# Attention, top-1 routing and a two-layer network in one kernel: where the first slot's row load and the w_in conversions stand

## The chip, the cores and the metric

The kernel runs on one core of one Trainium2 chip. The metric is device time in microseconds (us), the median of three timed runs; smaller is better. Nothing else runs on the chip.

## What is computed

The reference, cut to what matters here (all float32 unless said otherwise):

```python
# attention: 4 batches, 8 heads, 576 positions, head size 64
x = attention(q, k, v)                       # downsampled by 4 + a local band, summed
x = x.transpose(0, 2, 1, 3).reshape(2304, 512)
# one expert of eight for each token
e_idx = argmax(x @ w_gate + modality_bias[modality_id], axis=1)
for e in range(8):
    mask = e_idx == e
    h = np.maximum(x[mask] @ w1[e], 0.0)     # 512 -> 1024
    out[mask] = gate_w[mask, None] * (h @ w2[e])
# a dense network over all tokens; w_in (512 x 2048) and w_out arrive as float64
h = out @ w_in
g = np.maximum(h, 0.0) + alpha * np.minimum(h, 0.0)
return g @ w_out
```

## The kernel before

The program has three stages, one after the other on TensorE (PE).

**Attention and routing.** For each tile of 96 tokens the attention output is formed, the expert is chosen, and the row (512 values and its gate weight) is scattered by an indirect DMA into a table `xs` in device memory, sorted by expert. While this runs, five "early" blocks of 128 rows of the fullest expert are computed as filler (class `Early`: eight times an `ActivateRelu` of a first product, `eh<-ph`, then four copies `eo<-py` on ScalarE (ACT), then a store). At the end `Router.plan` works on one partition of VectorE (DVE): from the row counts it makes a table `r_tab` that says for each slot which expert and which rows it has, and a flag `r_rare` for a division of rows that does not fit the common case. The first slot's few numbers are cast into a small table of their own (`r_tab_109`) near the plan's start.

**Seven slots of 256 rows.** `slot(s)` takes 256 rows of one expert. Rows come by four DMAs (`L<-xs`, after a fill of zeros `xs<-z`), are scaled on GpSimd (POOL, `L<-L`), transposed on DVE (`T<-L`) and split into two fp32r parts: `xh` by a cast on ACT, `xl` by a subtraction on DVE (helper `split`). Weights are split in the same way: `w1h`, `w2h` on ACT, `w1l` on DVE, `w2l` on DVE or POOL. Each slot has 96 matmuls into `h` and 96 into `y`; ACT and DVE make `hh` and `hl` from `h`. A block that runs only if `r_rare` is set (`with tc.If(rare>0): every()`) stands between the stages, and all engines jump over it.

**The dense network**, five blocks of 512 rows (`moe2`), all PE.

w_in is float64. `W2in(i)` makes one of 32 pieces of 128 x 256: a DMA brings the raw words (`wi<-in_moe_w_in`, three buffers), three integer operations on DVE join them to a float32 (`xwi`, two buffers), ACT casts the high part (`wih<-xwi`) and POOL subtracts for the low part (`wil<-xwi,wih`). All 32 must be done before the dense network. `AT0=8` pieces are written in the program before the jump, six more in each of the slots 0 to 3.

Each engine takes its instructions in one order, fixed when the program is built; a scheduler sets it from the data dependencies and from priorities (`tc.high_priority`). DMAs are issued by SyncE (SP) in order too. Memory of a pool that is closed is given to pools opened later, and the first writer there waits for the last user of the old tile.

The functions that the change touches:

Of the kernel before, what the change touches and what calls it, by code (L numbers as in the profile page):

```python
# [8 lines left out]
B,H,S,D=4,8,576,64  # L9
# [6 lines left out]
def attention(ctx, tc, q, k, v, mod, wg, bias, xs, running, ps, eps, zeros, filler):  # L16
# [297 lines left out]
    def gate3(b,t):  # L314

        x,ng,oh=st.pop((b,t))
        p=psum([TT,E],f"rk{b}{t}")
        nc.tensor.matmul(p,lhsT=tri,rhs=oh,start=True,stop=False)
        nc.tensor.matmul(p,lhsT=ones,rhs=running[0],start=False,stop=False)
        nc.tensor.matmul(p,lhsT=ones[0:1],rhs=eoff,start=False,stop=True)  # L320
        old=running[0]
        running[0]=new_running(b*NT+t)
        nc.gpsimd.tensor_tensor(out=running[0],in0=old,in1=oh,op=ALU.add)
# [50 lines left out]
LEAD=1; WLOAD=tuple([0, 0, 1, 2, 2, 3, 3, 4]); EARLY=tuple([3, 6, 10, 14, 16]); AT0=8  # L374
F=1024; F2=2048; SL=256; SE=128; NSP=len(EARLY); NK=N//SL; NSU=-(-(N-SE*NSP)//SL); NSM=N//SL+E-1
ENG=mybir.EngineType

class Router:

    def __init__(self, tc, rp, cp):  # L380
# [18 lines left out]
        self.one=c([TT,1],"r_one",BF16); nc.gpsimd.memset(self.one,1.0)  # L399
        self.A=c([1,E,E],"r_A"); self.X=c([1,7,E],"r_X")  # L400
# [5 lines left out]
    def counts(self, psum, running):  # L406
        p=psum([1,E],"cnt")
        self.nc.tensor.matmul(p,lhsT=self.one,rhs=running[0],start=True,stop=True)
        return p
# [31 lines left out]
    def plan(self, psum, running, cp):  # L441
# [16 lines left out]
        nc.vector.tensor_tensor(out=left[:,0:1],in0=left[:,0:1],in1=dn,op=ALU.subtract)  # L458
# [25 lines left out]
        v=w([1,7,NSM,E],"v")  # L484
        nc.vector.tensor_tensor(out=v,in0=u[:,0:1].to_broadcast([1,7,NSM,E]),in1=X[:,:,None,:].to_broadcast([1,7,NSM,E]),op=ALU.mult)
        y=w([1,7,NSM],"y")
        nc.vector.tensor_reduce(out=y,in_=v,axis=AX.X,op=ALU.add)
# [49 lines left out]
def split(nc, hi, lo, x, lo_engine):  # L537

    nc.scalar.copy(hi,x)  # L539
    lo_engine.tensor_tensor(out=lo,in0=x,in1=hi.bitcast(F32),op=ALU.subtract)  # L540
# [11 lines left out]
class Rows:  # L552
# [26 lines left out]
class Early:  # L579
# [3 lines left out]
    def start(self, k, xr):  # L583
# [15 lines left out]
        for c in range(4):  # L599
            for f in range(8):  # L600
                S.append(lambda f=f,c=c: mm(("y",c),w.r2[:,f,128*c:128*c+128],h[:,f],f==0,f==7))
            S.append(lambda c=c: nc.scalar.copy(o[:,c],get(("y",c))))
# [5 lines left out]
def moe(tc, stack, router, wts, rows, ep, fp, W2in):  # L608
# [5 lines left out]
    xin={}  # L614
# [5 lines left out]
    def prep_x(s, name=""):  # L620
        L=xin[s]; T=rows.turn(wk,L,f"{name}{s}",SL)
        if name:
            hi=fp.tile([128,4,512],F32R,tag="xh",name=f"xh{name}{s}")[:,:,:SL]; lo=fp.tile([128,4,512],F32R,tag="xl",name=f"xl{name}{s}")[:,:,:SL]
        else:
            hi=wk.tile([128,4,SL],F32R,tag="xh",name=f"xh{name}{s}"); lo=wk.tile([128,4,SL],F32R,tag="xl",name=f"xl{name}{s}")
        split(nc,hi,lo,T,nc.vector)
        xin[s]=(hi,lo)
# [8 lines left out]
    W1={}; W2={}  # L636
# [36 lines left out]
    def slot(s):  # L673
        last=s+1==NSU
        if s==0: load_x(1)
# [11 lines left out]
        for f in range(8):  # L687
# [10 lines left out]
            nc.vector.scalar_tensor_tensor(out=hl,in0=h,scalar=0.0,in1=hh.bitcast(F32),op0=ALU.max,op1=ALU.subtract)  # L698
            H.append((hh,hl))
            if 2<=f<7: two(f-2)  # L700
            if f<6: W2in(AT0+6*s+f)
# [94 lines left out]
def body(tc,q,k,v,mod,wg,bias,w1,w2,w_in,w_out,alpha,out):  # L796
    nc=tc.nc
    with ExitStack() as ctx:
# [10 lines left out]
        with ExitStack() as a:  # L809
            cp=a.enter_context(tc.tile_pool(name="plan",bufs=1))  # L810
            router=Router(tc,rp,cp)
            running=[None]
# [16 lines left out]
            tmp=a.enter_context(tc.tile_pool(name="plan_work",bufs=1))  # L829
            with tc.high_priority(500): router.plan(psum,running,tmp)  # L830
# [17 lines left out]
        with ExitStack() as s1:  # L848
            def W2in(i):
                c,p=divmod(i,8); c=3-c; ps=slice(256*p,256*p+256)  # L850
                if c<0: return
                r=wst.tile([128,256,2],I32,tag="raw64",name=f"wi{c}{p}")
                nc.sync.dma_start(r.rearrange("p d w -> p (d w)"),w_in[128*c:128*c+128,ps].bitcast(I32))
                from64(nc,wst,f"wi{c}{p}",wir[:,c,ps],wil[:,c,ps],r,nc.gpsimd)
# [3 lines left out]
            first0()  # L858
            for i in range(AT0): W2in(i)
            with tc.If(rare>0): every()  # L860
# [33 lines left out]
```

## Time and profile before

| | us |
|---|---|
| median of three timed runs | 880.58 (879.72 to 883.82) |
| the profiled execution | 883.92 |
| its span | 882.2 |
| PE busy (92% of the span) | 814.7 |
| DVE busy (60%) | 530.3 |
| ACT busy (41%) | 360.6 |
| POOL busy (30%) | 261.8 |

A busy time is the sum of an engine's instructions over the whole span, across stages with different limits; what an engine waits for must be read from the stretch in question. In the rows further down a number in square brackets is the engine's idle time just ahead of an instruction, with what ended it.

### The profile page before, as it was taken

How to read it: one execution, taken by the hardware profiler on the slowest of the kernel's cores; microseconds unless marked ns; L12 is line 12 of the kernel's file. 1: busy time of each engine (PE TensorE's matmuls, PEld its weight loads, DVE VectorE, ACT ScalarE, POOL GpSimd, SP SyncE). 2: the span in 40 equal slices, each digit the busy share in tenths (PEclk: the TensorE clock that was granted, in tenths of full speed). 3: DMA queues.
4: the chain of work that ended last, by engine and by line, in shares of the span. 5: the costliest groups of instructions: out<-in, count | busy, mean ns of one | idle time of the engine just before them, and what ended most of it. 6: DMA issues, size and time to landing. Idle time of an engine off the chain costs nothing.

```text
span 882.2 us, 16794 instructions
## 1 busy us (share of the span) xinstructions
PE 814.7 (92%) x6175; PEld 698.2 (79%) x6175; DVE 530.3 (60%) x1302; ACT 360.6 (41%) x863; POOL 261.8 (30%) x450
## 2 busy tenths in 40 slices
PE   5787899899995699999999999999999999999997
PEld 3565687678895589889999888888888888888895
DVE  6856756656336799996755998443344333533361
ACT  8688795885322465565652233211121111111120
POOL 9325555365423645543321332100010001000100
PEclk9888789999999699999999999999999999999999
DMA  7635666322235434537401352200020001000000
GB/s 198 164 95 162 182 186 160 98 56 66 66 89 108 110 86 92 150 101 208 112 25 52 113 171 73 93 4 0 1 81 10 0 1 55 13 0 1 37 13 25
DMA packets 96611, 71.77 MB, mean 81 GB/s; under 512 B 40456, under 2 KB 83976, under 8 KB 96520
## 3 DMA queue, kind: packets, MB, share of 16 engines
q1 hardware_dynamic: 93544, 61.02, 25.8%
q0 software_dynamic: 2976, 9.59, 3.2%
q8 instruction: 51, 0.84, 0.4%
q14 instruction: 40, 0.33, 0.1%
HBM read 76.43 MB, written 18.90 MB: 108 GB/s over the span
## 4 chain that ended last, share of the span: by engine, by line
PE 57%; DVE 3%; DMA 2%; issue 2%; SPq 0%; POOL 0%; POOLq 0%; ACT 0%; DVEq 0%; ACTq 0%
PE oh L770 23%; PE oy L761 22%; PE h L695 7%; PE y L714 5%; DVE w2l L540 1%; DMA L<-xs 1%; DMA wi<-in_moe_w_in 1%; DVE w1l L540 1%; DVE xwi L548 1%; DVE hl L698 0%; DMA ytok<-L 0%; DMA oT<-ysT 0%; DMA out<-o,ti 0%; DVE xwi L549 0%; DVE oxl L540 0%
## 5 line engine op out<-in xcount | busy, mean ns | idle before, releaser
L539 ACT CAST gh<-m 128x512 fp32r<-128x512 f32 (+1 forms) x80 | 44.5, 556 | 241.6 <-DVE m L773 241.6
L770 PE MATMUL oh<-oxh,wil 128*128 128x512 f32 (+1 forms) x320 | 118.9, 372 | 0.0
L770 PE MATMUL oh<-oxh,wih 128*128 128x512 f32 (+1 forms) x320 | 118.9, 371 | 0.0
L770 PE MATMUL oh<-oxl,wih 128*128 128x512 f32 (+1 forms) x320 | 118.6, 371 | 0.0
L772 DVE TENSOR_SCALAR m<-oh,al 128x512 f32<-128x512 f32 (+1 forms) x80 | 55.5, 694 | 92.2 <-PE oh L770 92.2
L787 POOL DMA_INDIRECT out<-o,ti x18 | 17.6, 976 | 308.9 <-ACT o L786 271.3
L761 PE MATMUL oy<-woh,gh 128*128 128x512 f32 x272 | 107.1, 394 | 0.0
L761 PE MATMUL oy<-wol,gh 128*128 128x512 f32 x272 | 106.7, 392 | 0.0
L761 PE MATMUL oy<-woh,gl 128*128 128x512 f32 x272 | 106.4, 393 | 0.0
L695 PE MATMUL h<-xh,w1h 128*128 128x256 f32 x224 | 66.4, 297 | 15.2 <-DVE hl L698 7.9
L540 DVE TENSOR_TENSOR gl<-m,gh 128x512 fp32r<-128x512 f32 (+1 forms) x80 | 48.9, 612 | 40.1 <-ACT gh L539 40.0
L770 PEld LDWEIGHTS oh<-oxh,wil 128*128 128x128 f32 x320 | 60.2, 188 | 11.8
L770 PEld LDWEIGHTS oh<-oxh,wih 128*128 128x128 f32 x320 | 60.1, 188 | 11.5
L770 PEld LDWEIGHTS oh<-oxl,wih 128*128 128x128 f32 x320 | 60.1, 188 | 11.3
L695 PE MATMUL h<-xl,w1h 128*128 128x256 f32 x224 | 65.4, 292 | 0.0
L695 PE MATMUL h<-xh,w1l 128*128 128x256 f32 x224 | 65.1, 291 | 0.0
L714 PE MATMUL y<-hh,w2h 128*128 128x256 f32 x224 | 61.8, 285 | 0.7 <-ACT hh L697 0.7
L761 PEld LDWEIGHTS oy<-woh,gl 128*128 128x128 f32 x272 | 51.1, 188 | 12.0
L714 PE MATMUL y<-hl,w2h 128*128 128x256 f32 x224 | 59.6, 285 | 0.9 <-DVE hl L698 0.9
L714 PE MATMUL y<-hh,w2l 128*128 128x256 f32 x224 | 60.2, 285 | 0.0
L761 PEld LDWEIGHTS oy<-wol,gh 128*128 128x128 f32 x272 | 51.0, 188 | 11.4
L761 PEld LDWEIGHTS oy<-woh,gh 128*128 128x128 f32 x272 | 51.1, 188 | 11.0
(303 smaller groups left out, 1874.1 us busy)
## 6 DMA issues: line engine op xcount, KB each, us to landing
wraw<-in_moe_w SPq DMA_DIRECT2D x56, 512.0 KB
wi<-in_moe_w_in SPq DMA_DIRECT2D x32, 256.0 KB
wo<-in_moe_w_out SPq DMA_DIRECT2D x32, 256.0 KB
vw<-in_v SPq DMA_DIRECT2D x88, 64.0 KB
xs<-z SPq DMA_DIRECT2D x8, 528.0 KB
ldq<-in_q SPq DMA_DIRECT2D x16, 256.0 KB
ldk<-in_k SPq DMA_DIRECT2D x16, 256.0 KB
ldv<-in_v SPq DMA_DIRECT2D x8, 512.0 KB
```

Of the source, the lines that this page charges most:

```text
L539: nc.scalar.copy(hi,x)
L540: lo_engine.tensor_tensor(out=lo,in0=x,in1=hi.bitcast(F32),op=ALU.subtract)
L548: nc.vector.scalar_tensor_tensor(out=xi,in0=lw,scalar=29,in1=xi,op0=ALU.logical_shift_right,op1=ALU.bitwise_or)
L695: nc.tensor.matmul(h,lhsT=a[:,c],rhs=b[:,c],start=n==0,stop=n==11); n+=1
L714: nc.tensor.matmul(y,lhsT=a[:,f],rhs=b,start=n==0,stop=n==23); n+=1
L761: nc.tensor.matmul(y[t],lhsT=a[:,ts],rhs=b[:,f],start=f==0 and k==0,stop=f==15 and k==2)
L770: nc.tensor.matmul(h[:,:n],lhsT=a[:,c,fs],rhs=b[:,c,:n],start=k==0,stop=k==11); k+=1
L772: nc.vector.tensor_scalar(out=m[:,:n],in0=h[:,:n],scalar1=0.0,scalar2=al[:,f:f+1],op0=ALU.min,op1=ALU.mult)
L787: nc.gpsimd.indirect_dma_start(out=out[:],out_offset=bass.IndirectOffsetOnAxis(ap=ti[:,t:t+1],axis=0),in_=o[:],in_offset=None,bounds_check ...
```

## The change

Six edits. The plan's work tiles come out of the pool `plan` and no longer out of a pool opened for them (`plan_work`), and the table `v` of the plan is made in two parts. The load and preparation of the first slot's rows are traced at high priority. `AT0` goes from 8 to 4, so that slot 4 has the last four pieces of w_in. The pieces ahead of the jump are tied (`issue_after`) behind the first slot's load (on SP) and behind its `xl` (on DVE); those inside a slot are tied behind the `hl` of their step and behind the load of slot 1's rows. A raw piece of w_in is now loaded two pieces ahead of its conversion. Each engine gets one prefetch hint for the jump, placed behind an instruction of its own.

```diff
-LEAD=1; WLOAD=tuple([0, 0, 1, 2, 2, 3, 3, 4]); EARLY=tuple([3, 6, 10, 14, 16]); AT0=8
+LEAD=1; WLOAD=tuple([0, 0, 1, 2, 2, 3, 3, 4]); EARLY=tuple([3, 6, 10, 14, 16]); AT0=4
...
-        v=w([1,7,NSM,E],"v")
-        nc.vector.tensor_tensor(out=v,in0=u[:,0:1].to_broadcast([1,7,NSM,E]),in1=X[:,:,None,:].to_broadcast([1,7,NSM,E]),op=ALU.mult)
+        v=w([1,4,NSM,E],"v")
         y=w([1,7,NSM],"y")
-        nc.vector.tensor_reduce(out=y,in_=v,axis=AX.X,op=ALU.add)
+        for a,z in ((0,4),(4,7)):
+            nc.vector.tensor_tensor(out=v[:,:z-a],in0=u[:,0:1].to_broadcast([1,z-a,NSM,E]),in1=X[:,a:z,None,:].to_broadcast([1,z-a,NSM,E]),op=ALU.mult)
+            nc.vector.tensor_reduce(out=y[:,a:z],in_=v[:,:z-a],axis=AX.X,op=ALU.add)
...
     def first():
-        with tc.high_priority(0): load_x(0); L=xin[0]; prep_x(0)
+        with tc.high_priority(450): load_x(0); L=xin[0]; prep_x(0)
+        loaded=rows.loaded
         rows.tokens(L,router.reg(2,0,[ENG.SP],N),SL)
+        return loaded,turned[0]
...
-        if s==0: load_x(1)
+        if s==0: load_x(1); after[0]=rows.loaded
...
-            if f<6: W2in(AT0+6*s+f)
+            if f<6:
+                with tc.issue_after(d.ins), tc.issue_after(after[0].ins): W2in(AT0+6*s+f)
...
-            tmp=a.enter_context(tc.tile_pool(name="plan_work",bufs=1))
-            with tc.high_priority(500): router.plan(psum,running,tmp)
+            with tc.high_priority(500): router.plan(psum,running,cp)
+        early.go(len(early.steps)-10)
+        mark=early.mark
         early.finish()
...
+            def W2in_load(i):
+                c,p=divmod(i,8); c=3-c
+                if c<0: return
+                r=staged["in",i]=wst.tile([128,256,2],I32,tag="raw64",name=f"wi{c}{p}")
+                return nc.sync.dma_start(r.rearrange("p d w -> p (d w)"),w_in[128*c:128*c+128,256*p:256*p+256].bitcast(I32))
             def W2in(i):
+                W2in_load(i+2)
                 c,p=divmod(i,8); c=3-c; ps=slice(256*p,256*p+256)
-                if c<0: return
-                r=wst.tile([128,256,2],I32,tag="raw64",name=f"wi{c}{p}")
-                nc.sync.dma_start(r.rearrange("p d w -> p (d w)"),w_in[128*c:128*c+128,ps].bitcast(I32))
-                from64(nc,wst,f"wi{c}{p}",wir[:,c,ps],wil[:,c,ps],r,nc.gpsimd)
+                if c>=0: from64(nc,wst,f"wi{c}{p}",wir[:,c,ps],wil[:,c,ps],staged.pop(("in",i)),nc.gpsimd)
+            W2in_load(0); router.marks[ENG.SP]=W2in_load(1)
+            router.marks[ENG.Activation]=mark; router.marks[ENG.Pool]=running[1]
...
-            first0()
-            for i in range(AT0): W2in(i)
-            with tc.If(rare>0): every()
+            a=first0()
+
+            for e,i in router.marks.items():
+                with tc.issue_after(i.ins): tc.mark_branch_hint_location("rare",engines=(e,))
+            with tc.issue_after(a[0].ins), tc.issue_after(a[1].ins):
+                for i in range(AT0): W2in(i)
+            with tc.If(rare>0,label="rare"): every()
```

The order in which the built program issues its instructions changes at three places. First SP, from the raw loads of w_in behind the last tile's work to the load of the first slot's rows. Before:

```order
L853 DMA wi_4462<-in_moe_w_in 128x512
L853 DMA wi_4470<-in_moe_w_in 128x512
L853 DMA wi_4478<-in_moe_w_in 128x512
L512 TENSOR_LOAD r_tab_109 x2
L559 ISA
L559 DMA xs<-z 1024x1x132
L853 DMA wi_4486<-in_moe_w_in 128x512
L853 DMA wi_4494<-in_moe_w_in 128x512
L577 DMA ysT<-eo_3428 128x4x128
L512 TENSOR_LOAD r_tab_109
L564 ISA
L564 DMA L_4446<-xs 32x8x132
```

Of the change:

```order
L861 DMA wi_4412<-in_moe_w_in 128x512
L861 DMA wi_4414<-in_moe_w_in 128x512
L907 BRANCH_PREFETCH_HINT
L514 TENSOR_LOAD r_tab_109 x2
L561 ISA
L561 DMA xs<-z 1024x1x132
L514 TENSOR_LOAD r_tab_109
L566 ISA
L566 DMA L_4448<-xs 32x8x132
```

The two raw loads and the store that stood between the fill of zeros and the rows now come behind the rows.

Second ACT, the last instructions ahead of the jump: activations and copies of the last early block (`eh`, `eo`), the cast of the first slot's rows (`xh`) and casts of w_in (`wih`). Before:

```order
L598 ACTIVATE eh_3763<-ph_3924 128x128
L539 CAST wih<-xwi_4496 128x256
L602 COPY eo_3764<-py_4005 128x128
L539 CAST xh_4454<-T_4452 128x1024
L539 CAST wih<-xwi_4504 128x256
L602 COPY eo_3764<-py_4037 128x128
L539 CAST wih<-xwi_4512 128x256
L602 COPY eo_3764<-py_4047 128x128
L539 CAST wih<-xwi_4520 128x256
L602 COPY eo_3764<-py_4128 128x128
L539 CAST wih<-xwi_10130 128x256
L539 CAST wih<-xwi_10160 128x256
```

Of the change:

```order
L601 ACTIVATE eh_3763<-ph_3889 128x128
L541 CAST xh_4456<-T_4454 128x1024
L601 ACTIVATE eh_3763<-ph_3912 128x128
L601 ACTIVATE eh_3763<-ph_3918 128x128
L601 ACTIVATE eh_3763<-ph_3924 128x128
L541 CAST wih<-xwi_4471 128x256
L541 CAST wih<-xwi_4479 128x256
L605 COPY eo_3764<-py_4005 128x128
L605 COPY eo_3764<-py_4037 128x128
L541 CAST wih<-xwi_4487 128x256
L541 CAST wih<-xwi_4495 128x256
L605 COPY eo_3764<-py_4047 128x128
```

Behind these stand the copy `eo_3764<-py_4128`, the hint, the load of the flag and the branch. The cast of the rows has moved from behind the first copy to ahead of the sixth activation, and four casts of w_in stand ahead of the jump where ten stood.

Third DVE, its first instructions behind the jump: the low parts of slot 0's weights (`w1l`, `w2l`), the joining of w_in (`xwi`) and the first `hl`. Before:

```order
L549 SCALAR_TENSOR_TENSOR xwi_10193<-wi_10191,xwi_10193 128x256
L540 TENSOR_TENSOR w1l_0_10100<-wraw,w1h_0_10099 128x512
L547 TENSOR_SCALAR xwi_10228<-wi_10226 128x256
L540 TENSOR_TENSOR w1l_1_10104<-wraw,w1h_1_10103 128x512
L548 SCALAR_TENSOR_TENSOR xwi_10228<-wi_10226,xwi_10228 128x256
L540 TENSOR_TENSOR w1l_2_10108<-wraw,w1h_2_10107 128x512
L549 SCALAR_TENSOR_TENSOR xwi_10228<-wi_10226,xwi_10228 128x256
L540 TENSOR_TENSOR w2l_20_10346<-wraw,w2h_20_10345 128x512
L540 TENSOR_TENSOR w1l_3_10137<-wraw,w1h_3_10136 128x512
L698 SCALAR_TENSOR_TENSOR hl_0_10125<-h_0_10111,hh_0_10124 128x256
```

Of the change:

```order
L542 TENSOR_TENSOR w1l_0_10075<-wraw,w1h_0_10074 128x512
L542 TENSOR_TENSOR w1l_1_10079<-wraw,w1h_1_10078 128x512
L542 TENSOR_TENSOR w1l_2_10083<-wraw,w1h_2_10082 128x512
L542 TENSOR_TENSOR w2l_20_10321<-wraw,w2h_20_10320 128x512
L542 TENSOR_TENSOR w1l_3_10112<-wraw,w1h_3_10111 128x512
L704 SCALAR_TENSOR_TENSOR hl_0_10100<-h_0_10086,hh_0_10099 128x256
L549 TENSOR_SCALAR xwi_10105<-wi_4485 128x256
L550 SCALAR_TENSOR_TENSOR xwi_10105<-wi_4485,xwi_10105 128x256
L542 TENSOR_TENSOR w1l_4_10142<-wraw,w1h_4_10141 128x512
```

The joining of w_in now begins behind the first `hl`. Counted to the last `hl` of slot 3, DVE joins 22 and a third pieces of w_in and w_out behind the jump (before: 23 and a third); slot 4 joins five and two thirds more (before: none).

## Rows read from the trace of the kernel before

**Rows 1.** Busy time (count) by stretch: PE, PEld, DVE, ACT, POOL; clock, DMA.

```profile
280.00:300.00 20.00, 7.16 (x31) 6.84 (x32) 12.90 (x25) 7.52 (x17) 6.43 (x7) 0.61 0.42 133
```

**Rows 2.** Timeline of PE around the jump: start, duration, instruction, idle ahead.

```profile
255.64 7.41 PE L593 MATMUL py<-eh,wraw 128*128 128x128 f32 x64
...
268.38 3.84 PE L593 MATMUL ph<-Te,wraw 128*128 128x128 f32 x32 [2.65 <-ACT eh L598]
...
285.54 3.78 PE L593 MATMUL py<-eh,wraw 128*128 128x128 f32 x16 [6.20 <-ACT eo L602]
296.62 0.58 PE L695 MATMUL h<-xh,w1h 128*128 128x256 f32 x1 [7.31 <-ACT w1h L539]
```

**Rows 3.** Timeline of ACT around the jump.

```profile
283.97 1.04 ACT L539 CAST xh<-T 128x1024 fp32r<-128x1024 f32 x1 [7.91 <-DVE T L572]
...
289.36 0.27 ACT L602 COPY eo<-py 128x128 f32<-128x128 f32 x1
...
292.50 0.40 ACT L539 CAST wih<-xwi 128x256 fp32r<-128x256 f32 x1 [2.35 <-DVE xwi L549]
295.95 1.66 ACT L539 CAST w1h<-wraw 128x512 fp32r<-128x512 f32 x3 [3.05 <-ACTq L860]
```

**Rows 4.** Timeline of DVE from the plan to the jump.

```profile
260.78 0.29 DVE L547 TENSOR_SCALAR xwi<-wi 128x256 int32<-128x256 int32 x1 [2.90 <-DMA wi<-in_moe_w_in]
...
269.93 0.22 DVE L504 SCALAR_TENSOR_TENSOR r_tab<-r_xr,r_rf,r_yr 1x16 int32<-1x16 f32 x1
...
282.03 0.29 DVE L547 TENSOR_SCALAR xwi<-wi 128x256 int32<-128x256 int32 x1 [7.54 <-DMA wi<-in_moe_w_in]
...
282.70 1.24 DVE L572 STREAM_TRANSPOSE T<-L 128x1024 f32<-128x1024 f32 x1
...
295.81 0.43 DVE L549 SCALAR_TENSOR_TENSOR xwi<-wi,xwi 128x256 int32<-128x256 int32 x1 [3.01 <-DVEq L860]
```

**Rows 5.** Timeline of SP's DMA issues: ahead of the jump, behind it, in slot 3.

```profile
259.45 0.19 SPq L559 DMA_DIRECT2D xs<-z  x1
...
270.18 1.90 SPq L564 DMA_DIRECT2D L<-xs  x4
...
289.65 0.40 SPq L577 DMA_DIRECT2D ysT<-eo  x1
...
296.27 0.17 SPq L559 DMA_DIRECT2D xs<-z  x1
...
399.61 0.15 SPq L559 DMA_DIRECT2D xs<-z  x1
400.62 1.94 SPq L564 DMA_DIRECT2D L<-xs  x4
```

**Rows 6.** Timeline of POOL: the scaling of the first slot's rows.

```profile
275.75 1.91 POOL L570 TENSOR_TENSOR L<-L 128x1024 f32<-128x1024 f32 x1 [2.33 <-DMA L<-xs]
```

**Rows 7.** Busy time by stretch, as in Rows 1, just behind the jump.

```profile
296.60:301.40 4.80, 4.78 (x22) 4.76 (x23) 4.80 (x6) 3.93 (x8) 3.19 (x3) 0.50 0.76 200
```

**Rows 8.** The chain that ended last, in slot 6: start, duration, matmuls.

```profile
466.44 6.00 PE y L714 x50
```

**Rows 9.** Busy time by stretch: slots 0 to 3, then slot 4.

```profile
296.62:401.74 105.12, 96.72 (x744) 94.96 (x745) 100.88 (x170) 61.45 (x135) 53.24 (x43) 0.94 0.43 109
401.74:423.80 22.06, 20.90 (x175) 20.70 (x174) 12.70 (x23) 12.03 (x25) 7.43 (x5) 1.00 0.84 216
```

**Rows 10.** The same stretch, instructions on xwi alone: DVE, ACT, POOL.

```profile
296.62:401.74 105.12, 33.94 (x63) 8.86 (x22) 20.39 (x22) 0.94 0.43 109
```

**Rows 11.** DVE instructions on xwi behind the jump: ns min/median/max.

```profile
L549 DVE SCALAR_TENSOR_TENSOR xwi<-wi,xwi x22: 405/412/1521, 295.8 to 390.4; 128x256 int32<-128x256 int32 x22
...
L547 DVE TENSOR_SCALAR xwi<-wi x21: 244/282/1671, 297.2 to 387.8; 128x256 int32<-128x256 int32 x21
L548 DVE SCALAR_TENSOR_TENSOR xwi<-wi,xwi x21: 407/411/2142, 298.0 to 388.9; 128x256 int32<-128x256 int32 x21
```

**Rows 12.** DVE's longest wait for a raw piece inside the slots.

```profile
354.64 0.36 DVE L547 TENSOR_SCALAR xwi<-wi 128x256 int32<-128x256 int32 x1 [2.20 <-DMA wi<-in_moe_w_in]
```

More of the change, by code (lines that the diff above doesn't have):

```diff
@@ L322, in gate3 @@
         running[0]=new_running(b*NT+t)
-        nc.gpsimd.tensor_tensor(out=running[0],in0=old,in1=oh,op=ALU.add)
+        running[1]=nc.gpsimd.tensor_tensor(out=running[0],in0=old,in1=oh,op=ALU.add)
         jk=sm.tile([TT,E],F32,tag="jk",name=f"jk{b}{t}")
@@ L373, in attention @@
     loading.close()
-LEAD=1; WLOAD=tuple([0, 0, 1, 2, 2, 3, 3, 4]); EARLY=tuple([3, 6, 10, 14, 16]); AT0=8
+LEAD=1; WLOAD=tuple([0, 0, 1, 2, 2, 3, 3, 4]); EARLY=tuple([3, 6, 10, 14, 16]); AT0=4
 F=1024; F2=2048; SL=256; SE=128; NSP=len(EARLY); NK=N//SL; NSU=-(-(N-SE*NSP)//SL); NSM=N//SL+E-1
-ENG=mybir.EngineType
+ENG=mybir.EngineType; ENGINES=(ENG.Pool,ENG.Activation,ENG.PE,ENG.DVE,ENG.SP)
 class Router:
@@ L399, in __init__ @@
         self.one=c([TT,1],"r_one",BF16); nc.gpsimd.memset(self.one,1.0)
+        self.marks={}
         self.A=c([1,E,E],"r_A"); self.X=c([1,7,E],"r_X")
@@ L407, in counts @@
         p=psum([1,E],"cnt")
-        self.nc.tensor.matmul(p,lhsT=self.one,rhs=running[0],start=True,stop=True)
+        self.marks[ENG.PE]=self.nc.tensor.matmul(p,lhsT=self.one,rhs=running[0],start=True,stop=True)
         return p
@@ L457, in plan @@
         left=w([1,E],"left"); nc.vector.tensor_copy(left,nr[:,1])
-        nc.vector.tensor_tensor(out=left[:,0:1],in0=left[:,0:1],in1=dn,op=ALU.subtract)
+        self.marks[ENG.DVE]=nc.vector.tensor_tensor(out=left[:,0:1],in0=left[:,0:1],in1=dn,op=ALU.subtract)
         t=w([1,E,NK],"t2")
@@ L539, in split @@
     nc.scalar.copy(hi,x)
-    lo_engine.tensor_tensor(out=lo,in0=x,in1=hi.bitcast(F32),op=ALU.subtract)
+    return lo_engine.tensor_tensor(out=lo,in0=x,in1=hi.bitcast(F32),op=ALU.subtract)
 def from64(nc, pool, name, hi, lo, raw, lo_engine):
@@ L565, in load @@
             if n==SE: self.tc.add_to_no_dep_group("early rows",d.ins)
+        self.loaded=d
         return L
@@ L601, in start, with leave @@
                 S.append(lambda f=f,c=c: mm(("y",c),w.r2[:,f,128*c:128*c+128],h[:,f],f==0,f==7))
-            S.append(lambda c=c: nc.scalar.copy(o[:,c],get(("y",c))))
+            def leave(c=c): self.mark=nc.scalar.copy(o[:,c],get(("y",c)))
+            S.append(leave)
         S.append(lambda: r.store(o,SE*k,SE))
@@ L613, in moe @@
     yp=stack.enter_context(tc.tile_pool(name="m_y",bufs=3,space=PSUM))
-    xin={}
+    xin={}; turned=[None]
     def load_x(s, out=2, name=""):
@@ L625, in prep_x @@
             hi=wk.tile([128,4,SL],F32R,tag="xh",name=f"xh{name}{s}"); lo=wk.tile([128,4,SL],F32R,tag="xl",name=f"xl{name}{s}")
-        split(nc,hi,lo,T,nc.vector)
+        turned[0]=split(nc,hi,lo,T,nc.vector)
         xin[s]=(hi,lo)
@@ L635, in split2 @@
         return hi,lo
-    W1={}; W2={}
+    W1={}; W2={}; after=[None]
     def whole(s, e):
@@ L697, in slot @@
             nc.scalar.activation(out=hh,in_=h,func=AF.Relu)
-            nc.vector.scalar_tensor_tensor(out=hl,in0=h,scalar=0.0,in1=hh.bitcast(F32),op0=ALU.max,op1=ALU.subtract)
+            d=nc.vector.scalar_tensor_tensor(out=hl,in0=h,scalar=0.0,in1=hh.bitcast(F32),op0=ALU.max,op1=ALU.subtract)
             H.append((hh,hl))
             if 2<=f<7: two(f-2)
-            if f<6: W2in(AT0+6*s+f)
+            if f<6:
+                with tc.issue_after(d.ins), tc.issue_after(after[0].ins): W2in(AT0+6*s+f)
             if f==4 and not last: prep_x(s+1)
@@ L811, in body @@
             router=Router(tc,rp,cp)
-            running=[None]
+            running=[None,None]
             ps=a.enter_context(tc.tile_pool(name="a_psum",bufs=1,space=PSUM))
```

## The prediction

> **What bounds the kernel now.** I first read busy time by stretch, to find where PE, the engine with most work, stands still. It is the 20 us around the jump: PE is busy for 7.16 us of them [rows 1]. The slots behind are the second place, the dense network has no idle PE worth naming.
>
> Then I read the engines' timelines around the jump, each wait back to what ended it. PE waits three times: 2.65, 6.20 and 7.31 us, in all 16.2 us, and ACT ends each wait [rows 2]. For the 6.20 us, ACT's order holds the key: a copy that frees PE's accumulator stands behind the cast of the first slot's rows, and that cast waited 7.91 us for DVE's transposition [rows 3]. DVE in turn waited 7.54 us for a raw piece of w_in, which stands ahead of the transposition in its queue [rows 4], although the rows had been landed and scaled since 277.7 (275.75+1.91) [rows 6]. And the rows were late themselves: SP issued their load at 270.18, just when the plan's last instruction ended (269.93+0.22), 10.7 us after the fill of zeros [rows 4, 5]. The 7.31 us are more casts of w_in on ACT (the last ends at 292.90), then 3.05 us at the branch, then the first weight cast [rows 2, 3].
>
> In slots 0 to 3 DVE is busy for 100.9 of 105.1 us and PE is not the bound: four slots of 192 matmuls at 0.12 us (6.00/50) would be 92.2 us [rows 8, 9]. In slot 4 DVE is busy for 12.7 of 22.1 us and PE sets the pace [rows 9].
>
> **The change, part by part.** *Rows of the first slot.* The fill stays at 259.45: behind the scatter of the last tile, which the change does not touch. The load no longer waits for the plan, and no raw load or store stands between. In slot 3 the load follows the fill by 1.01 us (400.62-399.61), so it starts at 260.5 [rows 5]. From issue to the start of the scaling took 5.57 us (275.75-270.18), so the rows are there at 266.0 and scaled at 267.9 [rows 5, 6]. The plan itself loses its interleaved joining of w_in: one wait for a raw piece alone was 2.90 us [rows 4], so the plan ends by 267.3 (270.15-2.90) at the latest, and DVE is free when the rows are scaled. Transposition 1.24 us, to 269.2; `xh` 1.04 us, to 270.2 [rows 3, 4]; `xl` behind it. The plan's `v` in two parts costs one more instruction pair of some tenths of a us; it is hidden, because the rows land later.
>
> *PE up to the jump.* The last early block is 128 matmul passes (rows show 64 passes of the block before at 7.41 us, 0.116 us each); from the end of that block at 263.05 it needs 14.8 us, to 277.9 [rows 2]. In ACT's new order `xh` stands ahead of the sixth activation. That is ready about 268.6 (263.05 and 48 passes of 0.116 us), so PE loses some 1.6 us there, which takes the place of 2.65 and 6.20. The four joined pieces behind `xl` fall between 271.5 and 278 on DVE; their casts are ready before the third copy has to be. PE ends at 279.5, the last copy on ACT at 279.8. Before, ACT's last cast ended at 292.90: 13.1 us earlier. The fourth raw piece can only be issued when its buffer comes free near 273, and is wanted near 276; if DVE stood for it as long as it did for the worst one before (7.54 us [rows 4]), the two copies behind its cast would come some 3 us later. I take no such wait, since far fewer loads are under way.
>
> *The jump.* ACT stood for 3.05 us and DVE for 3.01 us [rows 3, 4]. Hints go early on DVE, PE, POOL and SP; ACT's stands directly ahead of its own flag load and branch, so it can prefetch almost nothing. I take the 3.05 us of ACT as unchanged: first cast at 282.8, PE at 283.5 (0.67 us later, as before), 13.1 us ahead of 296.62 [rows 2, 3]. From below, a hint that works gives 3 us more, 16.1. From above, and in place of that late piece, not on top of it, SP sets it: its first issue behind the jump came 6.6 us after its last store (296.27-289.65); from a store at 280.1 that is 286.7, hence 9.9 [rows 5]. I stay by ACT's row, since DVE and ACT, which end within 0.1 us of each other, show 3.0 us of their own queue.
>
> *Clock.* Behind the jump 22 matmuls ran in 4.80 us at a granted clock of 0.50 (the level of 1.2 GHz) [rows 7]; at the 0.12 us of the full clock they need 2.6 us [rows 8]. Before that, PE had stood still twice, for 6.20 and 7.31 us; now once, for some 4 us. Gain 0 to 2.2, I take 1.0.
>
> *Slots.* Joining one piece costs DVE 1.59 us there (33.94 us over 21 and a third pieces) [rows 10]. To the end of slot 3 there is one piece less: 1.6 us gained. Two-ahead loading can save the 2.20 us wait for a raw piece [rows 12]; I count half, 1.1, since DVE's queue has other waits next in line. Slot 4 gets 5.67 pieces, 9.0 us: DVE's 12.7 becomes 21.7 of 22.1 us [rows 9]. It just fits, but slots 0 to 3, as full as that, lost 3.2 us each ((105.1-92.2)/4); I take half, 1.7 lost. Net 1.0 gained; bounds: 3.8 gained (wait gone, slot 4 hidden) to 1.6 lost (no gain from the wait, slot 4 at its full 3.2).
>
> *Sum.* 13.1+1.0+1.0 = 15.1 us. The profiled execution took 883.92 us, so 868.8 by its own time; it was 3.3 us above the median of the runs shown, so 880.58-15.1 = 865.5 for the median. Bounds of the terms: 16.1+2.2+3.8 = 22.1 and 9.9+0-1.6 = 8.3, thus 858.5 to 872.3.
>
> *A rule against it.* The same joining costs 1.11 us by medians (0.282+0.411+0.412) and 1.59 us by the mean, and single instructions took up to 2.14 us instead of 0.41 [rows 10, 11]; DVE's operations with two operands stretch while POOL works. The change moves six pieces from the idle stretch ahead of the jump to slots in which POOL works too. The Trainium skill says of this ("SBUF — State Buffer", section "Who interferes with whom") that a DVE instruction with two SBUF inputs and a GpSimd instruction that reads SBUF exclude each other, and that the later one waits until the other has finished. By that rule moved pieces may cost DVE the other engine's whole instruction on top; the long rows agree with it. What it makes of the time stands as a rival below, priced from rows.
>
> **Rivals.** *Given back in the slots.* The six pieces that leave the stretch ahead of the jump find no slack, and each lengthens the slots by 1.59 us: 9.5 us given back instead of 1.0 gained, so 14.1-9.5 = 4.6 gained: 876.0. For it: DVE is the bound of slots 0 to 3 [rows 9]. Against it: counted in the new order, those slots have no more pieces than before, and slot 4's DVE stood idle for 9.4 us.
>
> *Slower: the shared-operand stall.* The same six pieces at the longest durations seen, 1.67+2.14+1.52 = 5.33 us each [rows 11], cost 32.0 us: 17.9 slower, 898.5. It decides from 14.1/6 = 2.35 us a piece, and is measurably slower from 3.1. The skill's rule on the two engines is what would bring this about. Against it: such durations are extremes in rows with medians of 0.28 to 0.41.
>
> *More than that.* The hints work on all engines and the early end of w_in's interference lets slots 0 to 3 run nearer PE's 92.2 us: half of their 12.9 us is 6.5, so 16.1+2.2+6.5 = 24.8, 855.8. For it: the first `hl` no longer has four joining operations ahead of it. Against: the hint on ACT stands too late, and DVE's total is nearly unchanged.
>
> *It does not do what it says.* The rows land as late as before, because the load waits for something other than the plan (the fill, or the last scatter); then ACT's `xh` holds up the sixth activation, ahead of all of the second product, so PE waits sooner and as long as before. Fewer casts ahead of the jump would be left: 880.6-2 = 878.5. Against: the old load began within 0.1 us of the plan's end.
>
> **How the numbers follow.** Chances: likeliest course 0.62 (its own range 858.5 to 872.3), more than that 0.11, given back 0.15, does not do what it says 0.06, slower 0.06. 0.5% of the time is 4.4 us, about what a measurement of this kernel can tell from no change. The rival at 876.0 lies near that edge (876.2); I count two thirds of it as faster. Faster 0.83, same 0.11, slower 0.06. The range 857 to 875 leaves out about half of each neighbouring case, some 0.06 below and 0.13 above.
>
> **What would show it.** The row load issues near 260.5 and the scaling starts near 266; PE's waits ahead of the jump shrink to under 2 us in all; ACT's first weight cast comes near 282.8, after a stand of about 3 us, PE's first slot matmul near 283.5. DVE's stand at the branch may fall under 1 us. Slots 0 to 3 take about 102 us, slot 4 about 24. Wrong would be: the load still behind the plan; a new long wait of ACT in the early block (`xh` or a cast of w_in ahead of a copy); SP behind the branch later than 285; or a slot 4 that takes 27 us or more.

## The result, and the profile after

The changed kernel takes 871.82 us (median of 4, 868.0 to 872.86) beside 882.2 us of the kernel before (median of 4, 879.72 to 884.5): ratio 0.9875, 95% interval 0.983 to 0.992. The profiled execution took 872.86 us, its span 871.1. Of the kernels further down, the one without the loads two ahead has its only profile from a slow execution (897.8 us, where that kernel's median is 886.36), whose rows are therefore not read.

Cut at three instructions, the two traces are easy to compare: the last count (`cnt`), the first product of slot 0, and the end of the last product of slot 6. Behind the last one both spans have 406.0 us left.

| | cnt at | slot 0 at | slots end | cnt to slot 0 | slots | sum |
|---|---|---|---|---|---|---|
| before | 255.55 | 296.62 | 476.24 | 41.07 | 179.62 | 220.69 |
| changed | 254.87 | 282.24 | 465.08 | 27.37 | 182.84 | 210.21 |
| difference | | | | -13.70 | +3.22 | -10.48 |

So slot 0 starts 13.7 us earlier, and the slots give 3.2 back. The other 0.7 us by which it starts earlier on the clock (296.62-282.24 = 14.4) lies ahead of the count, in code that the change leaves alone.

TensorE around the jump, which answers to [rows 2]: start, duration, instruction, idle ahead.

```profile
254.87 0.17 PE L409 MATMUL cnt<-running,r_one 96*1 96x8 bf16 x1
254.96 7.41 PE L596 MATMUL py<-eh,wraw 128*128 128x128 f32 x64
262.21 7.47 PE L596 MATMUL ph<-Te,wraw 128*128 128x128 f32 x64
269.52 7.31 PE L596 MATMUL py<-eh,wraw 128*128 128x128 f32 x64
282.24 0.58 PE L701 MATMUL h<-xh,w1h 128*128 128x256 f32 x1 [5.41 <-ACT w1h L541]
```

The waits of 2.65 and 6.20 us are gone: the last early block runs in one piece and ends at 276.83. One wait is left, 5.41 us at the jump. SP's issues, POOL, DVE and ACT in the same place, as in [rows 3 to 6]:

```profile
258.51 0.19 SPq L561 DMA_DIRECT2D xs<-z  x1
259.24 1.89 SPq L566 DMA_DIRECT2D L<-xs  x4
...
277.16 0.40 SPq L580 DMA_DIRECT2D ysT<-eo  x1
282.75 0.17 SPq L561 DMA_DIRECT2D xs<-z  x1
```

```profile
264.02 1.91 POOL L573 TENSOR_TENSOR L<-L 128x1024 f32<-128x1024 f32 x1 [8.07 <-DMA L<-xs]
```

```profile
262.93 0.22 DVE L506 SCALAR_TENSOR_TENSOR r_tab<-r_xr,r_rf,r_yr 1x16 int32<-1x16 f32 x1
265.97 1.25 DVE L575 STREAM_TRANSPOSE T<-L 128x1024 f32<-128x1024 f32 x1 [2.82 <-POOL L L573]
```

```profile
276.87 0.27 ACT L605 COPY eo<-py 128x128 f32<-128x128 f32 x1 [0.36 <-PE py L596]
281.57 0.62 ACT L541 CAST w1h<-wraw 128x512 fp32r<-128x512 f32 x1 [4.44 <-SPq L877]
```

The row load follows the fill by 0.73 us, where it followed it by 10.7 us before. ACT now stands 4.44 us at the branch, and the trace names SP as what ended it; before it was 3.05 us and its own queue [rows 3].

Busy time by stretch (PE, PEld, DVE, ACT, POOL, clock, DMA): slots 0 to 3, slot 4, slot 5, slot 6.

```profile
282.24:386.45 104.21, 95.77 (x728) 93.24 (x728) 96.56 (x166) 60.05 (x133) 54.34 (x43) 0.94 0.45 105
386.45:409.11 22.66, 22.55 (x188) 22.33 (x186) 20.07 (x38) 13.26 (x30) 12.32 (x10) 1.00 0.90 220
409.11:438.07 28.96, 26.43 (x219) 26.03 (x217) 22.74 (x40) 16.56 (x36) 9.13 (x7) 1.00 0.48 122
438.07:465.08 27.01, 27.01 (x223) 26.82 (x222) 9.93 (x19) 10.90 (x25) 4.71 (x4) 1.00 0.06 21
```

Against [rows 9], slots 0 to 3 read 0.9 us shorter and slot 4 0.6 longer. Slot 5 is new in the account. Before it read:

```profile
423.80:449.24 25.44, 25.44 (x215) 25.44 (x214) 17.55 (x27) 14.81 (x31) 8.42 (x5) 1.00 0.22 64
```

It grew by 3.5 us, with 40 operations on DVE for 27.

These stretches end at the first product (matmul) of the next slot, and some products of a slot come behind that mark: the lines count 728 products for 744 in slots 0 to 3, 188 for 175 in slot 4, 219 for 215 in slot 5. So they do not hold the same work. Cut at equal work instead, 192 products a slot from the first product of slot 0, they are:

| | slots 0 to 3 | slot 4 | slot 5 | slot 6 |
|---|---|---|---|---|
| before | 108.0 | 24.5 | 23.0 | 24.1 |
| changed | 109.1 | 23.5 | 26.1 | 24.1 |

So slots 0 to 3 are 1.1 us longer, not shorter, slot 4 is 1.0 us shorter, and slot 5 is 3.0 us longer. The whole stretch of the slots, from the first product to the last, needs no such cut. All instructions and then those on `xwi` alone (DVE, ACT, POOL), before:

```profile
296.62:476.24 179.62, 170.06 (x1349) 167.91 (x1350) 141.48 (x238) 99.73 (x215) 74.59 (x57) 0.97 0.39 103
```

```profile
296.62:476.24 179.62, 33.94 (x63) 8.86 (x22) 20.39 (x22) 0.97 0.39 103
```

and changed:

```profile
282.24:465.08 182.84, 171.77 (x1349) 168.42 (x1350) 149.29 (x259) 100.77 (x221) 80.51 (x63) 0.97 0.45 109
```

```profile
282.24:465.08 182.84, 43.95 (x84) 11.36 (x28) 25.41 (x28) 0.97 0.45 109
```

Twenty-one `xwi` operations (seven pieces) moved into the slots. They are 10.0 us of DVE there (43.95-33.94), DVE is busy 7.8 us longer in all, and the slots are 3.2 us longer. That the one causes the other is tested further down, with a mixed outcome.

The clock behind the jump (compare [rows 7]):

```profile
282.20:287.20 5.00, 4.96 (x23) 4.94 (x24) 3.17 (x5) 4.44 (x9) 3.37 (x3) 0.50 0.49 108
```

### The profile page after: what moved, and what is told of

Read it like the earlier page. It is cut to its first block, busy times and chain, and to the rows that moved or that the text cites. A ratio compares the mean times of both kernels' runs of the same rounds, so it can differ in the third digit from the quotient of the medians.

```text
span 871.1 us, 16800 instructions
## 1 busy us (share of the span) xinstructions
PE 813.2 (93%) x6175; PEld 696.5 (80%) x6175; DVE 529.4 (61%) x1304; ACT 361.4 (41%) x863; POOL 262.4 (30%) x450
## 4 chain that ended last, share of the span: by engine, by line
PE 51%; issue 1%; DVE 1%; DMA 0%; POOL 0%; ACT 0%; POOLq 0%; DVEq 0%
PE oh L777 23%; PE oy L768 22%; PE y L721 3%; PE h L701 3%; DMA out<-o,ti 0%; POOL L L573 0%; DVE xwo L550 0%; DVE hl L704 0%; POOLq L907 0%; DVE w1l L542 0%; DVE xwi L549 0%; ACT o L793 0%; DVE xl L542 0%; ACT wih L541 0%; ACT yo L724 0%
```

## The experiments

Each is timed against the kernel before, on its own chip. "cnt to slot 0" and "slots" are the stretches of the table above, from its profiled execution; the sum of both is free of what happened upstream.

| kernel | ratio, 95% interval | cnt to slot 0 | slots | sum |
|---|---|---|---|---|
| changed | 0.9875 (0.983 to 0.992) | 27.37 | 182.84 | 210.21 |
| no hints | 0.9859 (0.9805 to 0.9913) | 27.81 | 183.60 | 211.41 |
| store behind the jump | 0.9894 (0.9822 to 0.9966) | 27.38 | 183.97 | 211.35 |
| the same, no hints | 0.9899 (0.9864 to 0.9934) | 26.68 | 183.71 | 210.39 |
| w_out pieces late | 0.9874 (0.9801 to 0.9947) | 27.89 | 186.88 | 214.77 |
| no jump | 0.9903 (0.9867 to 0.9939) | | | 212.27 |
| rows alone | 1.0016 (0.9989 to 1.0043) | 38.32 | 181.22 | 219.54 |
| ties alone | 0.9984 (0.9951 to 1.0017) | 31.22 | 184.69 | 215.91 |
| no loads two ahead | 1.0015 (0.9987 to 1.0043) | | | |
| ties and loads two ahead | 0.9936 (0.9913 to 0.996) | 30.49 | 183.14 | 213.63 |
| six pieces ahead | 0.9940 (0.991 to 0.997) | 30.44 | 180.97 | 211.41 |
| eight pieces ahead | 0.9977 (0.9946 to 1.0008) | 32.56 | 186.34 | 218.90 |
| two pieces between | 0.9874 (0.9837 to 0.991) | 27.57 | 181.83 | 209.40 |

### What holds the jump

First theory (A): SP cannot leave the skipped block before the last store is in memory, and all wait for SP. Rival (B): each engine stands at the jump by itself. And the hints hide something, or not.

```diff
-            for e,i in router.marks.items():
-                with tc.issue_after(i.ins): tc.mark_branch_hint_location("rare",engines=(e,))
```

> The changed kernel without its five prefetch hints; every instruction else stands where it stood. Theory A (at the jump the last store's way to memory sets the time: SyncE leaves the branch 2.9 us after it gets there and the others are let go by SyncE, after 4.4 us on ScalarE; what each engine stands by itself lies inside that): ScalarE's first weight cast still ends 4.4 to 5.4 us after its last copy, and the kernel takes 872, at most 874. Theory B (the hints hide some 3 us of fetching at the jump, as ScalarE and VectorE stood 3.05 us there before): ScalarE waits about 7 us between its last copy and its first cast, and the kernel takes about 875.

ACT waited 4.22 us instead of 4.44, and the ratio is the same. The hints are worth nothing that shows here.

```diff
-        S.append(lambda: r.store(o,SE*k,SE))
+        self.last=lambda: r.store(o,SE*k,SE)
+        if k<NSP-1: S.append(self.last)
...
                 slot(s)
+                if s==0:
+                    with tc.issue_after(rows.after.ins): early.last()
```

(`rows.after` is the last load of slot 1's rows.)

> The changed kernel with one transfer moved: the store of the fifth early block, which stood last ahead of the jump on SyncE, is issued in slot 0 behind the loading of slot 1's rows. Nothing else moves. Theory A (the store's way to memory holds the jump): SyncE leaves the branch before ScalarE has done its last copy at about 277.1, ScalarE's wait falls from 4.44 us to its own share, 0.2 to 1.5 us with the hint, PE's first product of slot 0 goes from 282.2 to about 279, and the kernel takes 868.5 to 869.5. Theory B (each engine stands some 4 us at the jump by itself, whatever SyncE does): the start of slot 0 stays at 282.2 and the time at 872.

ACT, the last rows ahead of and behind the jump:

```profile
276.75 0.26 ACT L605 COPY eo<-py 128x128 f32<-128x128 f32 x1
281.09 0.27 ACT L605 COPY eo<-py 128x128 f32<-128x128 f32 x1 [4.08 <-ACTq L878]
```

The last copy now stands behind the branch, with no store left to wait for, and yet ACT stood 4.08 us, by its own queue. Slot 0 starts 27.38 us behind the count, as with the store ahead. (More moved than the expectation says: this last copy, and the order of the work in the slots.) Theory A falls. The reading is that what SP waits for with the store and what ACT stands by itself end at about the same time, so that taking away the one leaves the other.

Both together:

> The store behind the jump as in the run ahead, and no prefetch hints. If the hints hide a fetch that the store's way to memory covered until now, this is where they show: theory A gives ScalarE's stand at the jump 3 us as in the kernel before (3.05 us), the first product at about 281.5, and 871.5; against 869 with the hints. Rival: the hints are worth nothing, the two runs are alike within 0.5 us at the jump and in the time.

```profile
281.26 0.27 ACT L605 COPY eo<-py 128x128 f32<-128x128 f32 x1 [3.22 <-ACTq L876]
```

Without hints ACT's own stand is shorter, 3.22 us. Over the profiles that are read: where ACT's own queue ended the stand, it was 4.08 and 4.25 us with hints (the store behind, six pieces), and 3.04 to 3.22 without (before, this run, the ties alone, two pieces between). Where SP ended it, it was 3.22 to 4.79 either way. So the hints seem to cost ACT about 1 us where nothing hides it; what the stand consists of stays open.

The block taken out altogether (the path for inputs that fill more slots; this input does not take it), with its hints:

```diff
-            with tc.If(rare>0,label="rare"): every()
```

> The changed kernel without the conditional block that the jump skips (the path for inputs that fill more slots than are written out; this run's input does not take it) and without the hints for it. Measures what the jump costs in all. Theory B (every engine stands 3 to 4.5 us at the jump, with hints or without, with the store ahead or behind): TensorE's first product of slot 0 comes 0.8 to 1.8 us behind its last one of the early block, at 277.8 to 278.8, and the kernel takes 867 to 868.5. Rival (something else than the jump holds the first casts of the weights, such as the pools that open there): the product stays beyond 280 and the time at 870 or more.

Neither case came: without the block the scheduler mixes slot 0 with the last early block, so that slot 0's first product comes at 269.26, ahead of that block's last ones:

```profile
282.49 3.78 PE L596 MATMUL py<-eh,wraw 128*128 128x128 f32 x16 [4.44 <-ACT eo L605]
```

From the count to the slots' end it took 212.27 us, and the ratio is no better. This run does not price the jump, since the order changed too; it shows that taking the jump out does not by itself bring its 4 us back.

### Which part of the change brings the gain

The first slot's rows ahead and free of the plan, nothing else:

```diff
-            tmp=a.enter_context(tc.tile_pool(name="plan_work",bufs=1))
-            with tc.high_priority(500): router.plan(psum,running,tmp)
+            with tc.high_priority(500): router.plan(psum,running,cp)
...
-        with tc.high_priority(0): load_x(0); L=xin[0]; prep_x(0)
+        with tc.high_priority(450): load_x(0); L=xin[0]; prep_x(0)
```

(and `v` in two parts, as in the change)

> The kernel before with the first part of the change alone: the plan in the pool that outlives it, its product v in two parts, and the first slot's rows at the higher priority. Conversions, ties, loads and the jump stay as they were (32 xwi operations on VectorE ahead of the jump, where the changed kernel has 12). Theory A (the rows are what held TensorE ahead of the jump; the conversions only fill holes): slot 0 starts at 283 to 286, the slots take 179 as in the kernel before, and the kernel takes 869 to 872, no worse than the whole change. Theory F (what ties the conversions behind the slots is needed, too: 20 xwi operations ahead of the jump are some 9 us on VectorE, and they hold the jump): slot 0 starts at 288 to 292 and the kernel takes 874 to 879.

No gain: 1.0016. SP, ACT and PE, ahead of the jump:

```profile
265.67 1.53 SPq L853 DMA_DIRECT2D wi<-in_moe_w_in  x2
267.79 1.91 SPq L565 DMA_DIRECT2D L<-xs  x4
```

```profile
276.77 1.05 ACT L540 CAST xh<-T 128x1024 fp32r<-128x1024 f32 x1 [4.21 <-DVE T L573]
...
290.84 0.41 ACT L540 CAST wih<-xwi 128x256 fp32r<-128x256 f32 x1 [1.12 <-DVE xwi L550]
296.03 1.14 ACT L540 CAST w1h<-wraw 128x512 fp32r<-128x512 f32 x2 [4.79 <-SPq L860]
```

```profile
278.05 2.08 PE L594 MATMUL ph<-Te,wraw 128*128 128x128 f32 x8 [4.28 <-ACT eh L599]
296.70 0.58 PE L696 MATMUL h<-xh,w1h 128*128 128x256 f32 x1 [8.74 <-ACT w1h L540]
```

The rows are out of the plan's way, but raw loads of w_in still stand ahead of them on SP (the load starts 9.4 us behind the count, 4.4 in the changed kernel). And the ten casts of w_in run on to 291.25, 3.3 us after PE's last early product (287.97); only then can ACT jump. Even theory F, which named the conversions, expected a gain of 4 us or more; none came.

The other part alone, on the kernel before:

```diff
-            for i in range(AT0): W2in(i)
+            with tc.issue_after(a[0].ins), tc.issue_after(a[1].ins):
+                for i in range(AT0): W2in(i)
...
-            if f<6: W2in(AT0+6*s+f)
+            if f<6:
+                with tc.issue_after(d.ins), tc.issue_after(after[0].ins): W2in(AT0+6*s+f)
```

(with AT0=4, and the return values that it needs)

> The kernel before with the other part of the change alone: AT0=4 and the ties that keep the conversions behind the first slot's rows and behind the slots' own steps. The rows stay at the lower priority, the plan in its own pool (so that the rows' load waits for the plan's end), no loads two ahead, no hints. From the count (cnt) to the first product of slot 0 the kernel before takes 41.1 us, the changed one 27.4, the rows alone 38.3; the slots take 179.6, 182.8, and 181.2. Theory F (the conversions ahead of the jump are what held it; the earlier rows matter little by themselves): cnt to slot 0 29 to 31 us, slots 182.5 to 184.5, kernel 873 to 876. Rival G (both parts are needed, each alone brings little): cnt to slot 0 36 or more, 879 or more.

Slot 0 starts 9.9 us sooner behind the count, nearly as theory F said, but the time is that of the kernel before (0.9984). The profiled execution's sum is 4.8 us shorter than before; it was 2.9 us under its kernel's median (881.28 and 884.17 us), so part of that is the execution.

The changed kernel without the loads two ahead:

```diff
-            W2in_load(0); router.marks[ENG.SP]=W2in_load(1)
+            router.marks[ENG.SP]=rows.loaded
...
-                W2in_load(i+2)
+                W2in_load(i)
```

> The changed kernel with each piece of the second weight loaded when its own step is traced, not two pieces ahead. Theory F takes no part of the gain or of the longer slots from these loads: cnt to slot 0 27.4 to 28.5 (the first piece's load comes behind the rows', but VectorE has room), slots 182 to 185, kernel 871 to 873. Rival H (the loads two ahead crowd the rows' loads, and make the slots 3 to 4 us longer): slots 179.5 to 181, kernel 869 to 870. Rival I (without them VectorE waits for pieces in the slots): slots 186 or more, kernel 875 or more.

1.0015: rows, ties and hints are all there, and the whole gain is gone. The time is rival I's, by far more than it said; its mechanism, VectorE waiting for pieces in the slots, is not shown. The edit also puts the loads of the first two pieces behind the rows, and the scheduler set the order of work in the slots anew (on PE from the 62nd product on), so the run does not part the late loads from that order.

So both, ties and loads two ahead, on the kernel before:

> The ties with AT0=4 on the kernel before, as in the run with the ties alone, and the loads two pieces ahead added; the first slot's rows stay as they were before the change (lower priority, load behind the plan), no hints. The rows alone, the ties alone, and both without the loads two ahead each measured within 0.2% of the kernel before; all together measured 0.9875. Theory J (the loads two ahead are what the gain hangs on, because each load that a step waits for also holds SyncE and the row loads behind it; the earlier rows give only what the count-to-slot-0 time shows, 31.2 for 27.4 us): ratio 0.990 to 0.994, cnt to slot 0 30 to 31.5 us, slots 182 to 184. Theory K (the earlier rows are needed for any gain): ratio 0.997 or more. Theory L (the earlier rows are worth nothing at all, the loads two ahead all of it): ratio 0.986 to 0.988.

Theory J, at each of its three marks. Half of the gain needs nothing of the rows. SP's waits for the buffers of raw pieces inside the slots, with the ties alone and with the loads added (the largest row of each: us in total, times, longest):

```profile
SPq L857 <- DVE xwi L549: 24.8, 11, 5.8
```

```profile
SPq L857 <- DVE xwi L549: 20.8, 14, 3.3
```

Over all rows of that line SP waited 39.6 us in 17 waits with the ties alone and 30.6 us in 22 with the loads added; in the kernel before it was 17.7 us in 14, in the changed kernel 31.4 in 19. So most of this waiting came with that edit (the ties and AT0=4), and the loads two ahead go with a quarter less of it. That is how they would help: SP, which issues the rows and the weights too, is held for less at a stretch. It is argued from these rows, not shown by a run of its own; the order of work in the slots differs between these two runs as well. The loads two ahead without the ties were not run.

### What the slots give back

The two pieces of the second weight (`xwo`) that fell into slot 5, held back into slot 6:

```diff
-                from64(nc,wst,f"wo{f}{u}",woh[:,f,c],wol[:,f,c],staged.pop((f,u)),nc.gpsimd)
+                with tc.issue_after(slot.hold.ins): from64(nc,wst,f"wo{f}{u}",woh[:,f,c],wol[:,f,c],staged.pop((f,u)),nc.gpsimd)
```

(`slot.hold` is the third `hl` of slot 6)

> The changed kernel with the two pieces of the second weight that are converted early (xwo, 6 operations on VectorE, 4.0 us) held back from slot 5 to behind the third hl of slot 6; their loads stay. Theory C (slot 5 became 3.5 us longer, 28.96 for 25.44, because these operations and the L scaling beside them push hl of slot 5 back, on which PE waits 2.27 us): slot 5 takes 25.5 to 26.5, slot 6 at most 0.5 more, the kernel 869 to 870. Rival D (slot 5 is longer because its row load and the four w2l on GpSimd come in the same stretch, or the loads of weights come late): slot 5 stays at 28 to 29 and the time at 872.

From ACT's second copy of `yo` in slot 4 to that in slot 5 it took 23.7 us (417.90 to 441.64), in the changed kernel 24.0 (414.23 to 438.27), without hints 23.7, before 22.0. Theory C falls. Nor must slot 5 be the place of the loss: with the store behind the jump it took 22.2 us, with hints (417.82 to 440.02) and without, as before the change, and yet all slots together took 184.0 and 183.7. At equal work that run's loss lies ahead of slot 5 (110.6 us in slots 0 to 3, 25.8 in slot 4, 23.5 in slot 5). So where the slots lose goes with the order of their work. What made the slots of the run with `xwo` held back 4 us longer lies in slot 2, where its program is that of the changed kernel. POOL and DVE there:

```profile
337.34 1.92 POOL L573 TENSOR_TENSOR L<-L 128x1024 f32<-128x1024 f32 x1 [10.04 <-DMA L<-xs]
```

```profile
339.29 1.25 DVE L575 STREAM_TRANSPOSE T<-L 128x1024 f32<-128x1024 f32 x1 [5.54 <-POOL L L573]
```

and POOL in the changed kernel:

```profile
331.65 3.25 POOL L573 TENSOR_TENSOR L<-L 128x1024 f32<-128x1024 f32 x1 [4.46 <-DMA L<-xs]
```

The same row load, issued at 326.97 and 326.86, was there 10.4 us later in the one and 4.8 in the other.

Fewer pieces in the slots, with AT0=6 and AT0=8 in the changed kernel:

> The changed kernel with AT0=6: six pieces of the conversion traced ahead of the jump in place of four (18 xwi operations and 6 casts in front of it, for 12 and 4). Theory F (the slots became some 4 us longer, 182.6 to 185.8 from the first product to the last in four runs for 179.3, because six pieces more lie in them on VectorE): the jump moves back by 1 to 2 us, as the loads of two more pieces must come first, and the slots take 1 to 2 us less, so that the time stays at 872 within 1. Rival (the two pieces fit into the 7.3 us in which TensorE does the last early block and VectorE is idle): the start of slot 0 stays at 282.5, the slots take 1 to 2 us less, 870.

> The changed kernel with AT0=8 as before the change: 23 xwi operations and 6 casts ahead of the jump. By theory F the start of slot 0 goes to about 285 and the slots lose 3 us of their length, 872 again; by the rival (VectorE has room ahead of the jump) the start stays within 1 us of 282.2 and the time is 868 to 869. If the longer slots do not come from the pieces at all, they keep their 182.6 or more, and the time is 874 to 876.

With six, the slots are 1.9 us shorter than in the changed kernel, as theory F wanted, and the start of slot 0 is 3.1 us later, more than it wanted. ACT's last cast ahead of the jump, and its stand:

```profile
282.16 0.41 ACT L541 CAST wih<-xwi 128x256 fp32r<-128x256 f32 x1 [0.23 <-DVE xwi L551]
286.81 1.14 ACT L541 CAST w1h<-wraw 128x512 fp32r<-128x512 f32 x2 [4.25 <-ACTq L877]
```

The fifth and sixth piece end 2.8 us after PE (279.76), and the jump comes behind them. The ratio, 0.9940, is worse than the sum says (211.41 us, 1.2 more than the changed kernel): the profiled execution was 3.0 us under its kernel's median. With eight, the start goes back 5.2 us and the slots were not shorter but 3.5 us longer. That run does not bear theory F out; it comes nearest the third case of its expectation, in which the longer slots do not come from the pieces at all. I have no reading of it beyond two waits of PE for `hl`, 3.84 and 3.67 us.

A version that could have beaten the changed kernel: six pieces, two of them in the 2.82 us in which DVE waits for the scaling (store behind the jump, no hints):

```diff
+            with tc.high_priority(440), tc.issue_after(a[0].ins), tc.issue_after(router.end.ins):
+                for i in range(2): W2in(i)
             with tc.issue_after(a[0].ins), tc.issue_after(a[1].ins):
-                for i in range(AT0): W2in(i)
+                for i in range(2,AT0): W2in(i)
```

(`router.end` is the plan's last operation on DVE)

> A version that could beat the changed kernel: six pieces ahead of the jump as in the run with AT0=6, but the first two of them between the plan's last VectorE operation and the transpose T, where VectorE waits 2.8 us for the scaling on GpSimd; store behind the jump, no hints. By theory F the two pieces cost nothing there: cnt to slot 0 27 to 28 us (27.4 in the changed kernel, 30.4 with six pieces behind xl), slots 180.5 to 182 (181.0 with six pieces), kernel 868.5 to 870.5. Rival: the xwi operations and the scaling of L on GpSimd slow each other in that place, or the casts on ScalarE hold the relu that TensorE waits for; then cnt to slot 0 is 29 or more and the time 872 to 875.

Both stretches came as theory F said, 27.57 and 181.83 us, the shortest sum of all. The ratio is 0.9874, that of the changed kernel: 0.8 us is below what the timing tells. The time was not as theory F said: 874.01 us (the kernel before on the same chip: 883.96) for 868.5 to 870.5.

## Why the prediction was right in its direction, and where it was wrong

**What bounds the kernel** held: PE's stand around the jump, 16.2 us [rows 2], is 5.4 us now.

**Rows and PE up to the jump.** Load at 259.24 (predicted 260.5), scaling at 264.02 (266), PE's waits none (1.6 us), ACT's last copy done at 277.14 (279.8). Of the difference 0.7 us is upstream.

**The jump.** ACT's 3.05 us were taken as unchanged; it stood 4.44 us and SP ended it. The bound that I kept for SP, 9.9 us of gain, was too dark: SP's first issue came 5.6 us after its last store (282.75-277.16), not 6.6. An end 2.0 us earlier and a stand 1.4 us longer all but cancel: 13.7 us for the 13.1 of the sum, which is that close by luck.

**Clock**, 1.0 in the sum, measured 0: 23 matmuls in 5.00 us at a granted clock of 0.50 (the level of 1.2 GHz), after a wait of 5.4 us, and 22 in 4.80 us before [rows 7], after 7.3. With one wait of that length ahead of the slots the clock was as low behind the jump as with two. What the clock did give back lies ahead of the jump and was already in the 13.1: the last 16 passes of the early block took 3.78 us [rows 2] at a granted clock of 0.50, now 16 take 1.83 (7.31/4) at 1.00.

**Slots**, 1.0 gained in the sum, measured 3.2 lost: this term failed. The price of a piece was right (43.95/28 = 1.57 us, predicted 1.59; the 33.94 us are those of 63 operations, so of 21 pieces, which makes 1.62). At equal work, slots 0 to 3 lost 1.1 us where I took 2.7 as gained, slot 4 gained 1.0 where I took 1.7 as lost, and slot 5 lost 3.0. The count ended at slot 4, and slot 5 got the first two pieces of the second weight, which lay in slots 0 to 3 before. Held back, they left slot 5 nearly as long (23.7 us for 24.0 by the copies of `yo`), which speaks against them as what made it longer. What the 3.2 us come from stays open. Seven pieces more is the obvious reading, and six pieces ahead of the jump gave 181.0 and 181.8 us (182.8 in the changed kernel). But eight gave 186.3, and the rows alone, with the pieces where they were before, 181.2 beside 179.6, from one profile each.

With this term the whole sum is 13.7-3.2 = 10.5 us for 15.1. That forecast started from a median of 880.58 us, and the median of the result's runs is 882.2; these 1.6 us and the 4.6 us of the sum are nearly all that lies between 865.5 and 871.8.

**The rivals.** "Given back in the slots" had the right sign with too high a price: seven pieces, 10.0 us of DVE, beside slots 3.2 us longer; that the pieces cause it is not shown. The stall by shared operands did not come at its price: single operations stretch beside POOL, as here in slot 2 (DVE, then POOL), but the mean stays at 1.57 us a piece. The rule of the Trainium skill ("SBUF — State Buffer", section "Who interferes with whom") agrees with the second DVE row, which has two inputs. The first has one and is stretched as well, 1.30 us for a median of 0.28 [rows 11], so the rule on two inputs alone does not cover it. The stretching is common all the same: of the 84 `xwi` operations in the slots, the 50 that ran with POOL idle took at most 0.43 us, the 34 beside a POOL operation 0.78 us in the mean and up to 2.02.

```profile
336.87 1.30 DVE L549 TENSOR_SCALAR xwi<-wi 128x256 int32<-128x256 int32 x1
338.20 1.40 DVE L550 SCALAR_TENSOR_TENSOR xwi<-wi,xwi 128x256 int32<-128x256 int32 x1
```

```profile
336.71 4.04 POOL L542 TENSOR_TENSOR w2l<-wraw,w2h 128x512 fp32r<-128x512 f32 x3
```

**What it was due to.** Here the prediction was wrong although its time was not. It gave 13.1 us to the rows and the pieces behind them, and to the loads two ahead 1.1 us, half of the one wait that DVE shows for a raw piece [rows 12]. The runs say: rows alone nothing, ties alone nothing, both without the loads two ahead nothing, ties with the loads 0.64%, all 1.25%. So the step that failed is to read a load's worth from the wait of the engine that uses it. What the loads act through instead is not settled, as no profile of the kernel without them is read: it may be the queue that issues them, where rows and weights stand behind, or the order of work that the scheduler sets anew with them.

## What to carry to other kernels

Do not price a load that is moved by the wait of the engine that reads it alone; look also at what stands behind it on the queue that issues it, and at what else moves with it (here that path is argued, the price is measured). Parts of a change that each measure nothing can make the gain together, so undo them one at a time from the whole as well as trying each alone. Work moved out of a stall need not be free where it lands: follow every piece to the slot in which it ends, and compare stretches that hold the same work.

## What the runs showed of the hardware

- Leaving the skipped block cost ACT 3.04 to 4.79 us, and prefetch hints made it no shorter (4.44 with, 4.22 without; with the store behind 4.08 and 3.22).
- The same four row loads (132 KB each), in the same place of the same program, were followed by the scaling 4.8 us after their first issue in one execution and 10.4 us in another.
- The count, ahead of anything that the change touches, came between 254.13 and 261.25 us in twelve profiles. (The one that is not read and the one without the jump, whose order differs, are left out.) That is as much as most of these changes are worth, so the stretch behind it tells more than a single time.
